# The activation tile in two column halves, one store on another queue, and eight small scalings in another place: an attention and gated feed-forward kernel

## The chip, the core and the metric

The kernel runs on one core of a Trainium2 chip. The metric is the device time of one execution in microseconds (us), the median of several runs. The core has a matrix engine (TensorE, PE in the profile, with its weight loads as PEld), VectorE (DVE), ScalarE (ACT), GpSimd (POOL) and SyncE (SP). SP, ACT and POOL can issue DMA transfers, each on a queue of its own; the profile calls these SPq, ACTq and POOLq.

## The reference, cut to what matters

Attention with a decay per head comes first, in blocks over the sequence; its output for all heads is then the input of a gated feed-forward layer.

```
B, H, S, D = 4, 8, 768, 64              # batches, heads, positions, width of a head
# attention, per block: qb, kb, vb; Dmask[i,j] = lam**(i-j) for i >= j, else 0
intra = ((qb @ kb.T) * Dmask) @ vb
inter = (qb * lam**(pos+1)) @ kv_state
out   = intra + inter
kv_state = lam**block * kv_state + (kb * lam**(block-1-pos)).T @ vb
# feed-forward, on x = out as [3072 tokens, 512]
gate = 1 / (1 + exp(-(x @ w_gate)))     # w_gate, w_val: [512, 1536]
val  = x @ w_val
y    = (gate * val) @ w_out             # w_out: [1536, 512], y in float32
```

The attention doesn't depend on the size of its blocks; the kernel takes blocks of 128 positions.

## The kernel before, in words

**Tiling.** The sequence is cut into six steps `n` of 128 positions, with all four batches side by side: 512 tokens in a step. For each step the attention leaves its result transposed in the tile `XT[n]`: 128 partitions (features of a head pair), four feature groups `m`, four batches `b`, 128 positions `c`. `XT` is bf16 and has two buffers.

**Attention of a step.** q and k are transposed (on PE with `t_`, copied out by `e_q` on DVE and `e_k` on ACT into `QS` and `KS`, L255; from step 2 on by DMA transposes, `xbar`, issued by SP). `piece_s` (L277) makes the scores `sp`, `piece_m` multiplies them by the decay mask on DVE, `piece_i` (L297) and `piece_a` (L308) make the output `op` from the state `Sb` and from v, `piece_x` (L318) copies `op` into `XT`, and `piece_c` (L326) makes the new state from v and the decayed keys `KD`. `piece_kd` (L125) makes these on ACT: one small scaling for each head and, in step 1, each half of the batches.

**Feed-forward of a step.** `piece_gv` (L343) makes one of twelve tiles of 128 hidden features: the gate product `gp` and the value product `vp`, each four matmuls over the feature groups (L353), a sigmoid on ACT (`sg`, L366), and the product `ht` on DVE (L371). `gp`, `vp` and the output product `po` rotate through three PSUM buffers. The first tile of steps 0 and 1 is made in halves of 256 columns, so that its first half needs batches 0 and 1 alone. `piece_po` (L386) then makes the output for one batch from the twelve `ht`, copies it to `ob` (L390) and, from step 1 on, issues its store at once (L376, on SP). Step 0's stores are issued later. The last output of all is made in two parts: columns 0 to 383 are copied by DVE, 384 to 511 by ACT, and each part has its store.

**Order.** The order of instructions on every engine is written out by hand: nothing is rescheduled. A list `plan` holds the feed-forward units, each with attention pieces that are recorded behind it; every engine works off its own instructions in the order of recording. Step 0's output products are split into the lower and upper six hidden tiles (`lo`, `hi`), with step 1's attention between them (L542 to L549). Weights arrive on POOL's queue, in groups of one or two tiles (`load_g`, `load_v`), and step 0's feed-forward begins while they still arrive.

**Around the change.** ACT's order from step 0's upper output products on is: output copy of batch 0, four decays, output copy of batch 1, four decays, output copy of batch 2, k copy `KS` of batches 2 and 3, four decays, output copy of batch 3, XT copies. PE's order there is: output products of batches 0, 1 and 2 (upper half), transposes of k and q, lower output products of batch 3, scores of batches 2 and 3, upper output products of batch 3, then the rest of step 1's attention.

Of the kernel before, what the change touches and what calls it, by code (L numbers as in the profile page):

```python
# [8 lines left out]
FP32 = mybir.dt.float32  # L9
BF16 = mybir.dt.bfloat16  # L10
AF = mybir.ActivationFunctionType
# [5 lines left out]
def kernel(  # L17
# [11 lines left out]
    nc = tc.nc  # L29

    B, H, S, D = q.shape
    C = 128
    NSTEP = S // C
    HP = H // 2
    DM = H * D
    DFF = moe_w_gate.shape[1]
    NFT = DFF // 128
    NMT = DM // 128
    TCH = B * C
# [9 lines left out]
    xtp = ctx.enter_context(tc.tile_pool(name="xtp", bufs=2))  # L49
    htp = ctx.enter_context(tc.tile_pool(name="htp", bufs=2))  # L50
# [4 lines left out]
    ps_ff = ctx.enter_context(tc.tile_pool(name="ps_ff", bufs=3, space=bass.MemoryType.PSUM))  # L55
# [4 lines left out]
    FIRST_XBAR = 2  # L60

    WG = const.tile([128, NMT, DFF], BF16, tag="WG")
    WV = const.tile([128, NMT, DFF], BF16, tag="WV")
# [56 lines left out]
    def piece_kd(n, hs, parts=(0, 1)):  # L120
        for h in hs:
            for bs in ((0, B),) if n == 0 else [((0, NB2), (NB2, B))[i] for i in parts]:
                at = slice(*bs)
                i = slot(n, bs[0], h)
                nc.scalar.mul(KD[n][:, at, i, :], T_["k", n][:, at, i, :], kds[:, h:h + 1])  # L125
# [100 lines left out]
    QS, KS, MT, XT, SP, OP = {}, {}, {}, {}, {}, {}  # L226
# [55 lines left out]
    def piece_m(n, b):  # L282
        MT[n, b] = mtp.tile([128, 2, HP, C], BF16, tag="MT", name="MT")
        for u in range(2):
            nc.vector.tensor_tensor(out=MT[n, b][:, u], in0=SP[n, b][u],  # L285
                                    in1=(mask if n else mask0)[:, 1 - u if swapped(n, b) else u],
                                    op=ALU.mult)
# [24 lines left out]

    def piece_x(n, bs, eng=None):
        if n not in XT:
            XT[n] = xtp.tile([128, NMT, B, C], BF16, tag="XT", name="XT")
        for b in bs:
            e = eng or (nc.vector if n < FIRST_XBAR and b >= NB2 else nc.scalar)
            (e.tensor_copy if e is nc.vector else e.copy)(XT[n][:, :, b, :], OP[n, b])  # L318

    def piece_c(n, hps):  # L320
        cp = ps_at.tile([128, len(hps), B, 64], FP32, name="cp", tag="ps")
# [19 lines left out]
    HT = {}  # L341

    def piece_gv(n, ft):  # L343
        fs = slice(ft * 128, (ft + 1) * 128)
        x = XT[n].rearrange("p m b c -> p m (b c)")
        gp = ps_ff.tile([128, TCH], FP32, name="gp", tag="ff")
        parts = [slice(0, TCH)]
        if n < FIRST_XBAR and ft == 0:
            parts = [slice(0, TCH // 2), slice(TCH // 2, TCH)]

        def product(ps, W, part):
            for mt in range(NMT):
                nc.tensor.matmul(ps[:, part], lhsT=W[:, mt, fs], rhs=x[:, mt, part],  # L353
                                 start=(part is parts[0] and mt == 0),
                                 stop=(part is parts[-1] and mt == NMT - 1), skip_group_check=True)

        product(gp, WG, parts[0])
        if n == 0 and ft == 0:
            product(gp, WG, parts[1])
            parts = [slice(0, TCH)]  # L360
        elif len(parts) == 2:
            vp = ps_ff.tile([128, TCH], FP32, name="vp", tag="ff")
            product(vp, WV, parts[0])
            product(gp, WG, parts[1])
        sg = htp.tile([128, TCH], BF16, tag="sg", name="sg", bufs=3)
        nc.scalar.activation(sg, gp, AF.Sigmoid)  # L366
        if len(parts) == 1:
            vp = ps_ff.tile([128, TCH], FP32, name="vp", tag="ff")
        product(vp, WV, parts[-1])
        HT[n, ft] = htp.tile([128, TCH], BF16, tag="ht", name="ht", bufs=2 * NFT)  # L370
        nc.vector.tensor_mul(HT[n, ft], sg, vp)  # L371

    OB, PO = {}, {}

    def store(n, tt, c0=0, c1=DM):
        nc.sync.dma_start(out=out[tt * S + n * C:tt * S + (n + 1) * C, c0:c1],  # L376
                          in_=OB[n, tt][:, c0:c1])

    def piece_po(n, tt, c0, c1, eng, fts):
        if (n, tt) not in OB:  # L380
            OB[n, tt] = osb.tile([128, DM], FP32, tag="ob", name="ob")
        if fts[0] == 0:
            PO[n, tt] = ps_ff.tile([128, DM], FP32, name="po", tag="ff")
        po = PO[n, tt]
        for ft in fts:
            nc.tensor.matmul(po[:, :c1 - c0], lhsT=HT[n, ft][:, tt * 128:(tt + 1) * 128],  # L386
                             rhs=WO[:, ft, c0:c1], start=(ft == 0), stop=(ft == NFT - 1))
        if fts[-1] == NFT - 1:
            o = OB[n, tt][:, c0:c1]
            (eng.copy if eng is nc.scalar else eng.tensor_copy)(o, po[:, :c1 - c0])  # L390
            if n:
                store(n, tt, c0, c1)
# [46 lines left out]
    for b in range(3):  # L439
        piece_a(0, [b])  # L440
        piece_x(0, [b], nc.vector if b == 2 else nc.scalar)
    swap_halves()
    ops = [ps_at.tile([128, HP // 2, C], FP32, name="op", tag="ps") for _ in range(2)]
    for g in range(2):
        for hp in range(2 * g, 2 * g + 2):
            for w in range(2):
                nc.tensor.matmul(ops[g][rows_of(w), hp % 2, :], lhsT=T_["v", 0][:, 3, 2 * hp + w, :],
                                 rhs=MT[0, 3][:, w, hp, :], start=(hp % 2 == 0), stop=(hp % 2 == 1),
                                 skip_group_check=True)
    nc.scalar.copy(XT[0][:, 0:2, 3, :], ops[0])  # L450
    nc.vector.tensor_copy(XT[0][:, 2:4, 3, :], ops[1])
    nc.vector.tensor_copy(lamqs, lqs[0])


# [35 lines left out]
    def unit(f, *more):  # L490
        plan.append((f, list(more)))

    def gv(n, ft, *more):
        unit(lambda: piece_gv(n, ft), *more)

    def po(n, tt, *more, c=(0, DM), eng=nc.scalar, fts=range(NFT)):
        unit(lambda: piece_po(n, tt, *c, eng, fts), *more)

    def pair(f, n, bp):
        return lambda: f(n, [2 * bp, 2 * bp + 1])  # L500

    def m_(n, b):
        return lambda: piece_m(n, b)

    def trans(n, bp):
        def go():
            bs = [2 * bp, 2 * bp + 1]
            t_("k", n, bs)
            e_k(n, bs)
            t_("q", n, bs)  # L510
            e_q(n, bs)
        return go
# [7 lines left out]
    def att(n):  # L520
        def go():
            piece_i(n)
            piece_a(n, range(B))
            piece_x(n, range(B))
            if n < NSTEP - 1:
                piece_c(n, [0, 1])
                piece_c(n, [2, 3])
        return go

    def kd(n, h0, h1=None, **kw):  # L530
        return lambda: piece_kd(n, range(h0, h1 or h0 + 2), **kw)
# [9 lines left out]
    lo, hi = range(NFT // 2), range(NFT // 2, NFT)  # L541
# [1 line left out]
    po(0, 1, trans(1, 0), fts=lo)  # L543
    po(0, 2, pair(piece_s, 1, 0), m_(1, 0), m_(1, 1), kd(1, 0, 4, parts=[0]), fts=lo)
    po(0, 0, kd(1, 4, 8, parts=[0]), fts=hi)
    po(0, 1, kd(1, 0, 4, parts=[1]), fts=hi)
    po(0, 2, trans(1, 1), fts=hi)
    po(0, 3, kd(1, 4, 8, parts=[1]), pair(piece_s, 1, 1), m_(1, 2), m_(1, 3), fts=lo)
    po(0, 3, att(1), fts=hi)  # L549

    for n in range(1, NSTEP):
# [13 lines left out]
        if n == 1:  # L565
            more[5:] = [more[3], more[4], more[5], [], more[7], more[8], []]
            more[3], more[4] = [], []
            for i in range(4):
                more[7 + i].append(kd(nx, 2 * i))
            more[11] = [att(nx)]  # L570
            more[2].append(lambda: next_loads(2))
            more[3].extend([lambda tt=tt, j=j: store(0, tt, 256 * j, 256 * j + 256)
                            for tt in range(B) for j in range(2)])
            more[8].append(lambda: next_loads(3))
# [44 lines left out]
```

## Time and profile before

| What | Value |
|---|---|
| Time, median of three runs | 227.84 us (227.43, 227.84, 227.85) |
| Time of the profiled execution | 227.5 us |
| Its span, first to last instruction | 225.5 us |
| Instructions | 4170 |
| PE busy | 219.0 us, 97% of the span |
| ACT busy | 101.7 us, 45% |
| DVE busy | 101.9 us, 45% |
| PE's granted clock | 1.000 |
| `gp` and `vp` products of 512 columns, each | 379 ns |
| Output copy on ACT, 128x512 | 586 ns |
| Last store: issue to landing | 1.9 us |

Busy time is the time in which an engine has an instruction at work. Matmuls follow each other before the one ahead has ended, so the 379 ns of a product is its length, not the distance to the next. "Idle before" in the profile is time in which an engine waited, with the instruction of another engine or the DMA that ended the wait. The chain of waits is followed back from the last instruction, at each step to what released it.

### The profile page before, as it was taken

The page shows a single profiled execution, that of the slowest core. Times are in us where ns is not written, and L with a number is a line of the kernel's source. Part 1 is how long each engine was busy: PE and PEld are TensorE (multiplying, and loading weights), DVE is VectorE, ACT ScalarE, POOL GpSimd, SP SyncE. Part 2 cuts the span into 40 slices and gives each one's busy share as a digit, 9 for nine tenths or more (in the row PEclk, how much of TensorE's full clock was granted, in tenths as well). Part 3 has the DMA queues.
Part 4 walks back from the last instruction along what each step waited for, and adds up shares of the span by engine and source line. Part 5 has one row for each costly group of instructions (what it writes and reads, how often), then busy time and mean ns, then how long its engine had stood idle before and what let it go on. Part 6 is the DMA issues. An engine that isn't in the chain of part 4 may idle for free.

```text
span 225.5 us, 4170 instructions
## 1 busy us (share of the span) xinstructions
PE 219.0 (97%) x1675; PEld 107.0 (47%) x1675; DVE 101.9 (45%) x187; ACT 101.7 (45%) x216; POOL 64.0 (28%) x83
## 2 busy tenths in 40 slices
PE   7899999999999999999999999999999999999993
PEld 2554444557444644444644444644444544444442
DVE  4774542548468801488410488420378400334200
ACT  5877433684348623348523348532332342333220
POOL 7999854740192049006600030000000000000000
PEclk9999999999999999999999999999999999999999
DMA  7999999999999959993993958012100012100022
GB/s 114 151 170 183 196 202 178 171 157 155 235 170 156 177 166 138 198 198 40 156 159 124 203 37 60 0 49 93 47 0 3 0 49 93 47 0 0 3 93 94
DMA packets 106003, 25.18 MB, mean 112 GB/s; under 512 B 97152, under 2 KB 103552, under 8 KB 105984
## 3 DMA queue, kind: packets, MB, share of 16 engines
q0 software_dynamic: 82944, 13.90, 80.1%
q1 hardware_dynamic: 22896, 11.01, 20.2%
q8 instruction: 13, 0.21, 0.4%
q14 instruction: 6, 0.05, 0.1%
q10 hardware_dynamic: 144, 0.00, 0.0%
HBM read 28.32 MB, written 6.29 MB: 153 GB/s over the span
## 4 chain that ended last, share of the span: by engine, by line
PE 88%; POOL 4%; DMA 3%; ACT 2%; issue 1%; POOLq 0%
PE vp L353 27%; PE gp L353 27%; PE po L386 26%; DMA WV<-in_moe_w_val_dram 3%; PE sp L277 2%; PE op L308 2%; POOL vb L92 1%; PE op L297 1%; PE cp L326 1%; ACT kd L125 1%; POOL qb L92 1%; ACT ob L390 1%; POOL WG L103 1%; POOL kb L92 1%; ACT KS L255 0%
## 5 line engine op out<-in xcount | busy, mean ns | idle before, releaser
L371 DVE TENSOR_TENSOR ht<-sg,vp 128x512 bf16<-128x512 bf16 x72 | 49.5, 687 | 94.5 <-PE vp L353 94.5
L353 PE MATMUL gp<-XT,WG 128*128 128x512 bf16 (+1 forms) x296 | 74.2, 374 | 0.3 <-ACT XT L450 0.3
L353 PE MATMUL vp<-XT,WV 128*128 128x512 bf16 (+1 forms) x292 | 74.1, 376 | 0.1
L366 ACT ACTIVATE sg<-gp 128x512 bf16<-128x512 f32 x72 | 43.0, 597 | 66.6 <-PE gp L353 65.5
L386 PE MATMUL po<-WO,ht 128*128 128x512 bf16 (+2 forms) x300 | 63.9, 371 | 0.0
L353 PEld LDWEIGHTS <-WV 128*128 128x128 bf16 x292 | 28.5, 98 | 33.7 <-DMA WV<-in_moe_w_val_dram 0.6
L353 PEld LDWEIGHTS <-WG 128*128 128x128 bf16 x296 | 28.2, 98 | 32.4 <-DMA WG<-in_moe_w_gate_dram 0.5
L386 PEld LDWEIGHTS <-ht 128*128 128x128 bf16 x300 | 28.3, 98 | 31.9
L390 ACT COPY ob<-po 128x512 f32<-128x512 f32 (+1 forms) x24 | 13.7, 571 | 42.1 <-PE po L386 40.1
L285 DVE TENSOR_TENSOR MT<-sp,mask 128x512 bf16<-128x512 f32 x48 | 30.4, 683 | 3.0 <-PE sp L277 3.0
L125 ACT ACTIVATE kd<-kb,kds 128x128 bf16<-128x128 bf16 (+1 forms) x72 | 23.9, 403 | 0.0
L477 POOL COPY gates<-kt 128x1 bf16<-128x1 bf16 x4 | 0.8, 188 | 50.5 <-DMA kt<-kb 50.5
L92 POOL DMA_DIRECT2D vb<-in_v_dram x9 | 11.9, 1334 | 3.0 <-issue 1.2
L318 ACT CAST XT<-op 128x512 bf16<-128x512 f32 x20 | 10.4, 597 | 5.1 <-PE op L308 5.1
L335 DVE SCALAR_TENSOR_TENSOR Sb<-Sb,dec,cp 128x128 bf16<-128x128 bf16 x32 | 8.6, 342 | 3.2 <-PE cp L326 3.2
L98 POOL DMA_DIRECT2D qb<-in_q_dram x10 | 8.9, 912 | 2.5 <-DMA WO<-in_moe_w_out_dram 2.5
L98 POOL DMA_DIRECT2D kb<-in_k_dram x10 | 8.9, 895 | 1.8 <-DMA WO<-in_moe_w_out_dram 0.6
L92 POOL DMA_DIRECT2D qb<-in_q_dram x8 | 9.0, 1128 | 1.0 <-POOLq L603 0.8
L400 PE MATMUL zps<-Sb 128*128 128x512 bf16 x18 | 7.1, 539 | 1.5 <-DVE Sb L152 1.5
L92 POOL DMA_DIRECT2D kb<-in_k_dram x6 | 7.0, 1160 | 1.1 <-DMA WO<-in_moe_w_out_dram 0.6
L106 POOL DMA_DIRECT2D WV<-in_moe_w_val_dram x9 | 7.2, 811 | 0.0
L103 POOL DMA_DIRECT2D WG<-in_moe_w_gate_dram x8 | 6.4, 799 | 0.5 <-issue 0.5
(59 smaller groups left out, 86.7 us busy)
## 6 DMA issues: line engine op xcount, KB each, us to landing
out_dram<-ob SPq DMA_DIRECT2D x19, 256.0 KB, 2.0
vb<-in_v_dram POOLq DMA_DIRECT2D x4, 512.0 KB, 7.6
qb<-in_q_dram POOLq DMA_DIRECT2D x6, 256.0 KB, 9.1
kb<-in_k_dram POOLq DMA_DIRECT2D x6, 256.0 KB, 8.2
qb<-in_q_dram POOLq DMA_DIRECT2D x12, 128.0 KB, 8.8
WO<-in_moe_w_out_dram POOLq DMA_DIRECT2D x4, 384.0 KB, 12.3
kb<-in_k_dram POOLq DMA_DIRECT2D x10, 128.0 KB, 8.8
WG<-in_moe_w_gate_dram POOLq DMA_DIRECT2D x4, 256.0 KB, 6.8
```

Source lines behind the costliest of these rows:

```text
L92: nc.gpsimd.dma_start(out=T_[c, n][:, b0:nat], in_=src[b0:nat, :, sl, :].rearrange("b h s d -> s (b h) d"))
L98: nc.gpsimd.dma_start(out=T_[c, n][:, m:b1, u::2, :], in_=src[m:b1, 1 - u::2, sl, :].rearrange("b h s d -> s (b h) d"))
L103: nc.gpsimd.dma_start(out=WG[:, :, f0 * 128:f1 * 128], in_=wg_r[:, :, f0 * 128:f1 * 128])
L125: nc.scalar.mul(KD[n][:, at, i, :], T_["k", n][:, at, i, :], kds[:, h:h + 1])
L285: nc.vector.tensor_tensor(out=MT[n, b][:, u], in0=SP[n, b][u], in1=(mask if n else mask0)[:, 1 - u if swapped(n, b) else u], op=ALU.mult)
L318: (e.tensor_copy if e is nc.vector else e.copy)(XT[n][:, :, b, :], OP[n, b])
L335: nc.vector.scalar_tensor_tensor(out=Sb[:, hp, at, :], in0=Sb[:, hp, at, :], scalar=d[:, hp:hp + 1], in1=cp[:, i, at, :], op0=ALU.mult, op ...
L353: nc.tensor.matmul(ps[:, part], lhsT=W[:, mt, fs], rhs=x[:, mt, part], start=(part is parts[0] and mt == 0), stop=(part is parts[-1] and m ...
L366: nc.scalar.activation(sg, gp, AF.Sigmoid)
L371: nc.vector.tensor_mul(HT[n, ft], sg, vp)
L386: nc.tensor.matmul(po[:, :c1 - c0], lhsT=HT[n, ft][:, tt * 128:(tt + 1) * 128], rhs=WO[:, ft, c0:c1], start=(ft == 0), stop=(ft == NFT - 1))
L390: (eng.copy if eng is nc.scalar else eng.tensor_copy)(o, po[:, :c1 - c0])
```

## The change

Three edits. `XT` becomes a tile of two column halves, each with its four feature groups: batches 0 and 1 lie in the first half, 2 and 3 in the second. A half product reads 256 columns that lie together, as before; a whole product reads two runs of 256 columns that are 1024 elements apart. `gp` and `vp` are declared in the same two halves, both ahead of the products, and `piece_gv` goes through a list of products; the order of matmuls stays. The store of the very last part (batch 3 of the last step, columns 384 to 511) is issued by ACT. The eight decays of batches 2 and 3 of step 1 are recorded together behind the lower output products of batch 3, and so behind the k copy of batches 2 and 3.

```
     def piece_x(n, bs, eng=None):
         if n not in XT:
-            XT[n] = xtp.tile([128, NMT, B, C], BF16, tag="XT", name="XT")
+            XT[n] = xtp.tile([128, 2, NMT, TCH // 2], BF16, tag="XT", name="XT")
         for b in bs:
             e = eng or (nc.vector if n < FIRST_XBAR and b >= NB2 else nc.scalar)
-            (e.tensor_copy if e is nc.vector else e.copy)(XT[n][:, :, b, :], OP[n, b])
+            (e.tensor_copy if e is nc.vector else e.copy)(
+                XT[n][:, b // 2, :, b % 2 * C:(b % 2 + 1) * C], OP[n, b])
...
     def piece_gv(n, ft):
         fs = slice(ft * 128, (ft + 1) * 128)
-        x = XT[n].rearrange("p m b c -> p m (b c)")
-        gp = ps_ff.tile([128, TCH], FP32, name="gp", tag="ff")
...
+        gp, vp = (ps_ff.tile([128, 2, TCH // 2], FP32, name=c, tag="ff") for c in ("gp", "vp"))
+        sg = htp.tile([128, TCH], BF16, tag="sg", name="sg", bufs=3)
+        whole, first, second = slice(0, 2), slice(0, 1), slice(1, 2)
 
         def product(ps, W, part):
             for mt in range(NMT):
...
+                nc.tensor.matmul(ps[:, part], lhsT=W[:, mt, fs], rhs=XT[n][:, part, mt],
+                                 start=(part is not second and mt == 0),
+                                 stop=(part is not first and mt == NMT - 1), skip_group_check=True)
+
+        order = [(gp, WG, whole), (vp, WV, whole)]
+        if ft == 0 and n == 0:
+            order = [(gp, WG, first), (gp, WG, second), (vp, WV, whole)]
+        elif ft == 0 and n == 1:
+            order = [(gp, WG, first), (vp, WV, first), (gp, WG, second), (vp, WV, second)]
+        for ps, W, part in order:
+            product(ps, W, part)
+            if ps is gp and part is not first:
+                nc.scalar.activation(sg, gp.rearrange("p a b -> p (a b)"), AF.Sigmoid)
...
     def store(n, tt, c0=0, c1=DM):
-        nc.sync.dma_start(out=out[tt * S + n * C:tt * S + (n + 1) * C, c0:c1],
+        (nc.scalar if (n, tt, c1) == (NSTEP - 1, B - 1, DM) else nc.sync).dma_start(out=out[tt * S + n * C:tt * S + (n + 1) * C, c0:c1],
                           in_=OB[n, tt][:, c0:c1])
...
-    nc.scalar.copy(XT[0][:, 0:2, 3, :], ops[0])
-    nc.vector.tensor_copy(XT[0][:, 2:4, 3, :], ops[1])
+    nc.scalar.copy(XT[0][:, 1, 0:2, C:], ops[0])
+    nc.vector.tensor_copy(XT[0][:, 1, 2:4, C:], ops[1])
...
-    po(0, 1, kd(1, 0, 4, parts=[1]), fts=hi)
+    po(0, 1, fts=hi)
     po(0, 2, trans(1, 1), fts=hi)
-    po(0, 3, kd(1, 4, 8, parts=[1]), pair(piece_s, 1, 1), m_(1, 2), m_(1, 3), fts=lo)
+    po(0, 3, kd(1, 0, 8, parts=[1]), pair(piece_s, 1, 1), m_(1, 2), m_(1, 3), fts=lo)
```

More of the change, by code (lines that the diff above doesn't have):

```diff
@@ L344, in piece_gv @@
         fs = slice(ft * 128, (ft + 1) * 128)
-        x = XT[n].rearrange("p m b c -> p m (b c)")
-        gp = ps_ff.tile([128, TCH], FP32, name="gp", tag="ff")
-        parts = [slice(0, TCH)]
-        if n < FIRST_XBAR and ft == 0:
-            parts = [slice(0, TCH // 2), slice(TCH // 2, TCH)]
+        gp, vp = (ps_ff.tile([128, 2, TCH // 2], FP32, name=c, tag="ff") for c in ("gp", "vp"))
+        sg = htp.tile([128, TCH], BF16, tag="sg", name="sg", bufs=3)
+        whole, first, second = slice(0, 2), slice(0, 1), slice(1, 2)
@@ L351, in product @@
         def product(ps, W, part):
             for mt in range(NMT):
[L353 to L369, printed above, removed]
+                nc.tensor.matmul(ps[:, part], lhsT=W[:, mt, fs], rhs=XT[n][:, part, mt],
+                                 start=(part is not second and mt == 0),
+                                 stop=(part is not first and mt == NMT - 1), skip_group_check=True)
@@ L370, in piece_gv @@
+        order = [(gp, WG, whole), (vp, WV, whole)]
[7 more added lines that the diff above has]
+                nc.scalar.activation(sg, gp.rearrange("p a b -> p (a b)"), AF.Sigmoid)
         HT[n, ft] = htp.tile([128, TCH], BF16, tag="ht", name="ht", bufs=2 * NFT)
-        nc.vector.tensor_mul(HT[n, ft], sg, vp)
+        nc.vector.tensor_mul(HT[n, ft], sg, vp.rearrange("p a b -> p (a b)"))
```

## The prediction

> **What bounds the kernel now.** I read the busy times first, then the list of PE's waits, then the chain of waits in order of time, and last the timeline of the two places that the chain points at.
>
> ```profile
> PE 219.0 (97%) x1675; PEld 107.0 (47%) x1675; DVE 101.9 (45%) x187; ACT 101.7 (45%) x216; POOL 64.0 (28%) x83
> PE zps L400 <- DVE Sb L152: 1.5, 1, 1.5
> PE sp L277 <- ACT KS L255: 0.5, 1, 0.5
> PE gp L353 <- ACT XT L450: 0.3, 1, 0.3
> PE tk L234 <- DVE kb L260: 0.2, 1, 0.2
> ```
>
> PE is busy for 219.0 of 225.5 us, and the other four lines are all the waits its matmuls have (us in total, times, longest). Three of them lie before 16 us. The table of stages says the same of the rest: between 48.6 and 221.9 us PE is busy for 173.26 of 173.30 us. So a gain can only come from ahead of 18 us, from the one wait near 48 us, from a matmul's own length, or from behind the last matmul.
>
> ```profile
> 12.11 5.84 DMA WV<-in_moe_w_val_dram
> 18.00 1.04 PE vp L353 x4
> ...
> 44.39 1.17 ACT kd L125 x4
> 45.56 0.47 ACT ob L390
> 46.03 1.18 ACT kd L125 x4
> 47.20 0.47 ACT ob L390
> 47.67 0.92 ACT KS L255
> 48.59 0.05 issue
> 48.64 0.62 PE sp L277 x16
> ```
>
> This is the chain of waits (start, length, what). The first two lines: the value product of the second feed-forward tile starts when its 128 columns of WV have landed, at 18.00, whatever PE did before. The last seven: at 44 to 48.6 the chain leaves PE and runs through ACT, because the k copy (KS) of batches 2 and 3 stands behind four key decays (kd) and two output copies.
>
> ```profile
> 47.29 0.69 DVE L244 TENSOR_TENSOR QS<-tq,lamq 128x1024 bf16<-128x1024 bf16 x1 [2.63 <-PE tq L234]
> ...
> 221.86 0.33 SPq L376 DMA_DIRECT2D out_dram<-ob  x1
> 221.94 0.27 ACT L390 COPY ob<-po 128x128 f32<-128x128 f32 x1 [2.03 <-PE po L386]
> ...
> 222.71 0.34 SPq L376 DMA_DIRECT2D out_dram<-ob  x1
> ```
>
> From the timeline. The q copy that the same scores need is ready at 47.98, ahead of KS (48.59). At the end the last output copy is done at 222.21, but its store leaves SP only at 222.71, since SP issued the store before it from 221.86 to 222.19.
>
> ```profile
> L353 PE MATMUL vp<-XT,WV 128*128 128x512 bf16 x284 | 72.9, 379 | 0.1
> L353 PE MATMUL gp<-XT,WG 128*128 128x512 bf16 x280 | 71.9, 379 | 0.0
> ```
>
> The groups kept apart by shape: 564 whole products are PE's largest work, and all read XT.
>
> [...]four products in 0.864 us, 216 ns each.[...] No operation of the kernel before moves data through PE in two runs[...].[...] SP's little semaphore instruction ends at 222.22, the copy it waits for at 222.21, and still 0.49 us pass before the store.[...]
>
> **The change, part by part.** Durations are of the profiled execution: span 225.5, time 227.5, so 2.0 us lie around the span. The median of the three runs shown is 227.84, 0.34 above it; I take the sum off the median.
>
> *Layout of XT.* It adds and removes no instruction. In the two built programs each half product waits for the same copies as before: the first four for ACT's second copy of XT, those of the second half for the copies of batches 2 and 3. Thus the layout takes no wait away. What it saves: nothing. Even if block 0's first tile began earlier, the cover is WV's landing at 18.00: PE starts the second gate product at 16.89, ends it 0.86 later at 17.75, and waits 0.25. If that cover were gone, the 0.30 us in front of the first product would be the most to gain. In block 1 the first half starts at 52.74 without a recorded wait. The XT copies write runs of 128 elements as before, with a smaller step between them; ACT's (597 ns, four runs) take what a sigmoid takes (597 ns, one run), so I cost those at nothing. What it may cost: 564 whole products now read two runs. Lower bound 0[...] . I take 0, as ACT's four-run writes pay nothing.
>
> *gp and vp as tiles of two halves, taken together.* The buffers rotate in the same order; the matmuls keep order and number. PE loses some waits on its own earlier matmuls and three small semaphore instructions, and gains a few such waits. All concern matmuls at least 28 PE instructions back, so done: 0 both ways.
>
> *k copies ahead of decays.* On ACT four kd (1.27 us) leave the place before the output copy of batch 2, and join the other four behind KS. New times: the 18 output products from 42.30 end as before; the last starts at 45.98 and ends 0.38 later at 46.36, so the output copy runs 46.40 to 46.99. The k transposes end at 46.80. KS, which overlaps the copy before it by 0.09, runs from 46.90 to 47.91, 0.68 earlier. PE needs it later than that: its last output product starts at 48.16, and elsewhere scores follow such a product by 0.305 (41.435 to 41.74). So scores start at 48.16 + 0.305 = 48.47 instead of 48.64, **0.17 us** earlier; the 0.5 in the list counts from another point. QS (47.98) and KS (47.91) both make it, with half a microsecond to spare. What is late next on ACT: eight kd of 0.29 to 0.32 from 47.8, done by 50.4. The next output copy, 50.70 before, is due at 50.53; the state products need the decays at 52.0. No DMA is moved past. Block 0's stores are issued from 59.24 on, behind SP's transposes, so earlier copies move none of them. Behind 48.6 PE has no other gap, so 0.17 reaches the end. Bounds: 0 to 0.17.
>
> *Last store on ACT's queue.* SP loses one issue and one semaphore instruction; ACT gains one issue behind its last copy, with nothing queued behind it but the end. On SP a store waiting for its copy left 0.03 after it (221.83 to 221.86). [...]the issue can start at 222.21 + 0.03 = 222.24: 0.47 earlier. Landing follows 1.9 after the start, and about 0.9 of closing follows that. Bytes follow an issue by 0.8 (the DMA rates show those of the 192 KB store from 222.7 to 223.4), so the small store's would start near 223.06 and share the last 0.3 us of those; I take 0.02 off: **0.45 us**. Floor: [...]222.21 + 0.49 = 222.70, gain 0. Below nothing: ACT's only earlier DMA took 0.43 to issue and 3.1 to land, against 0.34 and 1.9; 1.2 - 0.47 = 0.73 slower. I don't take it: that one was a broadcast load at the start beside two others, and SP's first issue took 0.46 as well. Ceiling: the 192 KB store lands at 221.86 + 1.9 = 223.76, 0.85 before the last one did.
>
> Sum: 0 + 0 - 0.17 - 0.45 = **-0.62 us**: 226.9 against the profiled 227.5, **227.2** against the median.
>
> **Rivals.**
> *The store gains nothing*[...]. For it: SP's 0.49 of silence. Against: SP had to issue another store right before. Then only 0.17 is left: 227.67. Chance 0.20.
> *The scores find another wait*, so that only the store counts: the output copy, now right behind its products, holds KS past 48.47. Against it speaks the half microsecond of room. 227.84 - 0.45 = 227.39, within the bound. Chance 0.10.
> *Two-run reads slow PE.* The place is each of the 564 whole products, with no cover as PE is full.[...] It cancels the gain at 0.62 / 564 = 1.1 ns and makes the kernel slower by 0.2% (0.46 us, about what a measurement can tell from no change) from 1.9 ns on. For it: XT's reads are the one thing changed in PE's bulk, and untried here. Against: ACT's strided writes are free. Chance 0.08.
> *The change does not do what it says*: the layout frees no wait, as shown; that is already in my forecast.
>
> **How the numbers follow.** My forecast has chance 0.62, at 227.2 with 227.0 to 227.4 of its own. Faster 0.62; the first two rivals make "within 0.2%", 0.30; the third slower, 0.08. The range 226.85 to 227.85 holds the forecast, both rivals inside 0.2%, and the 0.4 us by which the three runs shown differ; left out are the slow reads and part of the tails.
>
> **What would show it.** Right: whole gp and vp products still 216 ns apart; no wait of sp at L277 for KS, with kd x8 behind KS on ACT; the last store on ACT's queue at about the end of its copy, its landing near 224.2, a span near 224.9; 18.00 unchanged for the second value product. Wrong: a product spacing above 217 ns, an ACT store issued 0.4 us or more behind its copy, or landing later than 2.2 us, or a new PE wait behind 48 us.

## The result, and the profile after

The changed kernel takes 226.89 us, median of four runs (226.46 to 227.10), against 227.78 for the kernel before (four runs, 227.43 to 227.85). The ratio is 0.9962 with a 95% interval of 0.9944 to 0.9979: 0.89 us less by the medians, 0.5 to 1.3 by the interval. A second measurement gave 226.84 against 227.71, ratio 0.9956 (0.9943 to 0.9969). The profiled execution took 226.46 us with a span of 224.5, 1.0 us less than the span before. It was the fastest of its four runs, 0.43 under their median; the profiled execution before took 227.5, 0.28 under its own. So the two profiles overstate the gain by about 0.15 us. One execution of all those used below, one of the decays alone, took 582.44 us, and the figures of that kernel leave it out.

Lines of `piece_gv` and all behind it stand some lines further up in the changed file: L353 is L352 there, L386 is L381, L390 is L385, L376 is L371. First PE's busy time from the page, and the list of its matmuls' waits (us in total, times, longest), of the changed kernel.

```profile
PE 217.7 (97%) x1675; PEld 106.9 (48%) x1675; DVE 101.9 (45%) x187; ACT 101.7 (45%) x216; POOL 63.9 (28%) x83
PE zps L395 <- DVE Sb L152: 1.5, 1, 1.5
PE tq L234 <- DMA qb<-in_q_dram: 0.7, 1, 0.7
PE tk L234 <- DVE kb L260: 0.6, 1, 0.6
PE sp L277 <- ACT KS L255: 0.5, 1, 0.5
PE gp L352 <- ACT XT L445: 0.3, 1, 0.3
```

The line of `sp` and `KS` is still there. That is a correction to the prediction, which took it for the wait near 48 us. It is the wait of a much earlier `sp`, and was so before, so that all four waits listed in the prediction lie ahead of 16 us. This is the timeline of the kernel before at that place:

```profile
9.25 0.40 PE L277 MATMUL sp<-QS,KS 64*128 64x128 bf16 x8 [0.47 <-ACT KS L255]
```

The wait near 48 us stands with the weight loads, since the scores' weights are what comes from `KS`. The list of PEld's waits, first of the kernel before, then of the changed one:

```profile
PEld L277 <- ACT KS L255: 1.2, 2, 0.6
```

```profile
PEld L277 <- ACT KS L255: 0.6, 1, 0.6
PEld L277 <- ACT kd L125: 0.4, 1, 0.4
```

Of the two waits for `KS` one is left, and a line of 0.4 us with `kd` as its releaser has come in. The weight loads of the scores in question are these in the timeline, first before, then after:

```profile
48.63 0.45 PEld L277 LDWEIGHTS <-KS 64*128 64x128 bf16 x16 [0.58 <-ACT KS L255]
```

```profile
48.23 0.45 PEld L277 LDWEIGHTS <-KS 64*128 64x128 bf16 x16 [0.42 <-ACT kd L125]
```

The weight loads of the scores of batches 0 and 1, which in the kernel before wait for no other engine there, look like the second:

```profile
41.74 0.45 PEld L277 LDWEIGHTS <-KS 64*128 64x128 bf16 x16 [0.42 <-issue]
```

So 0.42 us passes there in any case. `kd` is named as the last thing on ACT by the profile, but these loads read `KS`, not `kd`, so I take it for no wait. What is gone is the rest, 0.58 - 0.42 = 0.16. The chain of waits of the changed kernel shows the place itself (start, length, what), and ACT's timeline beside it what ACT does there now.

```profile
46.12 0.45 PE tk L234 x8
46.56 0.45 PE tq L234 x8
47.01 1.29 PE po L381 x6
48.31 0.55 PE sp L277 x16
```

```profile
46.15 0.58 ACT L385 COPY ob<-po 128x512 f32<-128x512 f32 x1 [0.36 <-PE po L381]
46.64 1.02 ACT L255 COPY KS<-tk 128x1024 bf16<-128x1024 bf16 x1
47.54 2.44 ACT L125 ACTIVATE kd<-kb,kds 128x128 bf16<-128x128 bf16 x8
50.30 0.58 ACT L385 COPY ob<-po 128x512 f32<-128x512 f32 x1 [0.31 <-PE po L381]
```

The chain no longer leaves PE there: `KS` and the decays are gone from it. `KS` is done at 47.66, and the eight decays end at 49.98, before the next output copy is due. Whole products, which now read two runs, keep their distance, 0.86 us for four: first the chain before, then after.

```profile
23.35 0.86 PE vp L353 x4
24.21 0.86 PE gp L353 x4
```

```profile
55.11 0.86 PE vp L352 x4
55.97 0.86 PE gp L352 x4
```

At the end of the kernel, by the timeline:

```profile
221.46 0.33 SPq L371 DMA_DIRECT2D out_dram<-ob  x1
221.54 0.27 ACT L385 COPY ob<-po 128x128 f32<-128x128 f32 x1 [2.04 <-PE po L381]
221.84 0.35 ACTq L371 DMA_DIRECT2D out_dram<-ob  x1
```

The last store leaves 0.03 us behind its copy, where it left 0.50 behind it before.

**Where the 1.0 us of the two spans came from.** The last copy ends 0.40 earlier (221.81 for 222.21). Of this, 0.16 arose at the scores: from the first of the six lower output products to the scores it is 48.24 - 46.85 = 1.39, before 48.64 - 47.09 = 1.55. The other 0.24 was there ahead of them; the next section takes it for scatter of the first loads, not for a gain of the change. From the end of the last copy to the end of the span it is 2.72, before 3.29: 0.57. Together 0.40 + 0.57 = 0.97.

### The profile page after: what moved, and what is told of

The parts are those of the page before. It is cut to its first block, busy times and chain, and to the rows that moved or that the text cites. A ratio compares the mean times of both kernels' runs of the same rounds, so it can differ in the third digit from the quotient of the medians.

```text
span 224.5 us, 4166 instructions
## 1 busy us (share of the span) xinstructions
PE 217.7 (97%) x1675; PEld 106.9 (48%) x1675; DVE 101.9 (45%) x187; ACT 101.7 (45%) x216; POOL 63.9 (28%) x83
## 4 chain that ended last, share of the span: by engine, by line
PE 92%; POOL 3%; DMA 2%; issue 1%; ACT 0%; POOLq 0%
PE gp L352 28%; PE po L381 28%; PE vp L352 28%; PE sp L277 2%; DMA vb<-in_v_dram 2%; PE op L308 2%; PE op L297 1%; PE cp L327 1%; POOL qb L92 1%; POOL vb L92 1%; POOL kb L92 1%; PE tq L234 0%; PE tk L234 0%; ACT XT L445 0%; PE op L442 0%
## 5 line engine op out<-in xcount | busy, mean ns | idle before, releaser
L352 PE MATMUL gp<-XT,WG 128*128 128x512 bf16 (+1 forms) x296 | 74.2, 374 | 0.3 <-ACT XT L445 0.3
L352 PE MATMUL vp<-XT,WV 128*128 128x512 bf16 (+1 forms) x292 | 74.1, 376 | 0.0
L381 PE MATMUL po<-WO,ht 128*128 128x512 bf16 (+2 forms) x300 | 64.0, 371 | 0.0
L352 PEld LDWEIGHTS <-WV 128*128 128x128 bf16 x292 | 28.5, 98 | 33.6 <-DMA WV<-in_moe_w_val_dram 0.4
L352 PEld LDWEIGHTS <-WG 128*128 128x128 bf16 x296 | 28.2, 98 | 32.4 <-DMA WG<-in_moe_w_gate_dram 0.5
L381 PEld LDWEIGHTS <-ht 128*128 128x128 bf16 x300 | 28.3, 98 | 32.0 <-issue 0.2
L385 ACT COPY ob<-po 128x512 f32<-128x512 f32 (+1 forms) x24 | 13.7, 571 | 42.0 <-PE po L381 42.0
L395 PE MATMUL zps<-Sb 128*128 128x512 bf16 x18 | 6.3, 482 | 1.5 <-DVE Sb L152 1.5
```

The source lines that it names most:

```text
L352: nc.tensor.matmul(ps[:, part], lhsT=W[:, mt, fs], rhs=XT[n][:, part, mt], start=(part is not second and mt == 0), stop=(part is not first ...
```

## Experiments

Two questions were open: whether the layout has any part in the gain, and why the end of the kernel gave 0.57 where the earlier issue alone gives 0.47. Unless said otherwise each kernel is compared with the kernel before on the same chip in five rounds.

### The layout alone

The kernel before with the first edit only (XT, gp and vp in two halves; store on SP, decays as before).

> The kernel before with the column halves of XT, gp and vp alone; store on SP and decays as before. My theory (the layout takes no wait away and two-run reads are free): 0 us, within 0.15 of the kernel before; whole products still 216 ns apart (four in 0.86 us); the last store on SP still about 0.5 us behind its copy; scores at L277 still held by KS. Rival A (the layout is what brought the 0.3 us that the sum did not hold): 0.25 to 0.3 us faster. Rival B (two-run reads cost): slower, 0.56 us for each ns a product.

Measured: 227.68 against 227.71 us, ratio 0.9995 (0.9985 to 1.0004). It is worth nothing that can be told: the interval goes from 0.34 us faster to 0.09 slower. Whole products keep their 0.86 us for four. Its second value product started at 18.34, *later* than the kernel before's 18.00, and in the changed kernel it started at 17.69. Over the profiles with the new layout the start is 18.34, 17.69, 17.81 and 17.97 (the last with XT in four runs, a kernel further down); over those without it, 18.00, 18.11, 17.97, 17.99, 17.97 and 18.09. In eight of these ten profiles the start waits for the landing of WV, which is at 17.64 in the changed kernel's and at 17.77 to 18.06 in the others; in two (the layout alone, 18.34, and all but the layout, 18.09) WV landed earlier, at 17.90 and 17.66, and the start waits for the products ahead of it, which were late behind the landing of a block of v. So the start follows when the first loads land, and it scatters by some 0.6 us; WV landed at 17.66 without the layout too. I take the 0.24 in front of the scores for this scatter. Rival B is out. Rival A's 0.25 to 0.3 us lies just inside the interval; its start should have been earlier, and this profile shows it later.

### The store alone

```
     def store(n, tt, c0=0, c1=DM):
-        nc.sync.dma_start(
+        (nc.scalar if (n, tt, c1) == (NSTEP - 1, B - 1, DM) else nc.sync).dma_start(
...
```

> The kernel before with the last store alone on ACT's queue. My theory: the store starts 0.03 us behind its copy instead of 0.50, so 0.45 to 0.5 us faster. Rival A: the closing behind the store also gets shorter (0.13 us in the profile of the changed kernel), so 0.6 us faster. Rival B: part of the gain is lost to the transfer that it now overlaps: 0.3 us or less.

Measured: 227.06 against 227.71 us, ratio 0.9969 (0.9957 to 0.9981), so 0.65 us less (0.43 to 0.98 by the interval, whose lower end is about the predicted 0.45). The store starts at 222.35, 0.03 behind its copy, and from the end of the copy to the end of the span it is 2.74 us, before 3.29: 0.55, so that more than the start shortened, as rival A had it. The store starts where the prediction had it; the size of the gain was put too small.

### The decays alone

```
-    po(0, 1, kd(1, 0, 4, parts=[1]), fts=hi)
+    po(0, 1, fts=hi)
     po(0, 2, trans(1, 1), fts=hi)
-    po(0, 3, kd(1, 4, 8, parts=[1]), pair(piece_s, 1, 1), m_(1, 2), m_(1, 3), fts=lo)
+    po(0, 3, kd(1, 0, 8, parts=[1]), pair(piece_s, 1, 1), m_(1, 2), m_(1, 3), fts=lo)
```

> The kernel before with the eight decays behind the k copy alone. My theory: scores start 0.30 to 0.31 us behind the last output product instead of 0.48, so 0.16 to 0.17 us faster, and no more. Rival: by being earlier the rest of step 1 on ACT frees something else, 0.3 us or more; then PE would show another gap closed behind 48 us.

Measured: 227.59 (thirteen runs) against 227.71 us, ratio 0.9993 (0.9984 to 1.0001). By the ratio 0.16 us, by the medians 0.12: the time agrees with the theory, and with nothing as well. The trace is clearer: from the first lower output product to the scores it is 1.40 us (47.05 to 48.45), as in the changed kernel, where the two kernels above without this edit have 1.55 and 1.54. No other gap behind 48 us closes.

### The changed kernel again

> The changed kernel once more, unchanged. My theory: the parts add to 0.62 to 0.65 us, and the 0.89 of the first measurement held some 0.25 of scatter of the landing of the first loads: 0.55 to 0.75 us faster here. Rival: the extra is real, 0.85 us or more.

Measured: 226.84 against 227.71 us, ratio 0.9956 (0.9943 to 0.9969): 0.87 us. This expectation failed, and its rival held: the interval, 0.71 to 1.30 us, leaves out 0.62. The three parts measured alone add to 0.03 + 0.65 + 0.12 = 0.80 by medians, and most of what the prediction lacked is in the store.

### All but the layout

The kernel before with both the store and the decays.

> The kernel before with the store on ACT's queue and the decays behind the k copy, and XT, gp and vp as before: all of the change but the layout. The changed kernel was 0.87 us faster than the kernel before in its second measurement (interval 0.71 to 1.3). Theory (the layout is worth nothing, also beside the others): 0.75 to 0.9 us faster, ratio 0.996 to 0.9967. Rival (the layout helps only once the rest is in place): 0.6 us faster or less.

Measured: 227.00 against 227.79 us, ratio 0.9964 (0.9950 to 0.9977): 0.79 us, within what the theory gave. Its interval, 0.52 to 1.14, holds the rival's 0.6 as well. The layout adds nothing that these intervals can tell beside the other two edits either.

### The two last stores with queues exchanged

Is SP itself slow, or is it SP with another issue just behind it? SP here issues the small store alone; ACT issues the large one.

```
-            if n:
+            if n and (n, tt, c1) != (NSTEP - 1, B - 1, 384):
                 store(n, tt, c0, c1)
+            if (n, tt, c1) == (NSTEP - 1, B - 1, DM):
+                store(n, tt, 0, 384)
...
-        nc.sync.dma_start(
+        (nc.scalar if c1 == 384 else nc.sync).dma_start(
...
```

> The kernel before with the queues of the two last stores exchanged: SP issues the small one (64 KB) and, with no other issue ahead of it in the last microsecond, ACT issues the larger one (192 KB) behind its own last copy. Theory[...]: SP's small store starts 0.02 to 0.05 us behind its copy. Rival: SP is slow by itself, 0.4 us or more. As to the time: the 192 KB now start about 0.4 us later than before, beside the 64 KB; [...]the gain is below that of the store alone: 0 to 0.4 us faster.

Measured: 227.08 against 227.87 us, ratio 0.9970 (0.9959 to 0.9981): as good as the store on ACT. The timeline of the end:

```profile
221.94 0.27 ACT L390 COPY ob<-po 128x128 f32<-128x128 f32 x1 [2.03 <-PE po L386]
221.94 0.35 ACTq L376 DMA_DIRECT2D out_dram<-ob  x1
222.23 0.33 SPq L376 DMA_DIRECT2D out_dram<-ob  x1
```

SP's store starts at 222.23, 0.02 behind its copy (222.21). So SP is not slow by itself: this store has no other issue of SP just ahead of it, where in the kernel before 0.52 us passed behind the large store's (222.19 to 222.71). One issue behind another does not take that long everywhere: among the eight stores of step 0, from 59.24 us on in the kernel before, 0.04 to 0.10 us lies between the end of one issue and the start of the next. What sets the 0.52 was not shown. My guess on the large store was wrong: ACT does not hold it until its own copy is done. It starts together with that copy at 221.94, 0.08 later than SP issued it before and not 0.4, so this run could not show whether a late large store lands late as well.

### The store late on ACT's queue

The store alone, but ACT makes its last copy three times, so that the store leaves as late as SP's did.

```
-            (eng.copy if eng is nc.scalar else eng.tensor_copy)(o, po[:, :c1 - c0])
+            for _ in range(3 if (n, tt, c1) == (NSTEP - 1, B - 1, DM) and c0 else 1):
+                (eng.copy if eng is nc.scalar else eng.tensor_copy)(o, po[:, :c1 - c0])
```

> The kernel before with the last store on ACT's queue, and ACT's last output copy made three times over, so that the store is issued 0.5 to 0.65 us behind the end of the first of them: no earlier than SP issued it (0.50), but on ACT's queue. The store alone was 0.65 us faster than the kernel before; its earlier start explains 0.47 of it. Theory A (the rest is time[...]): landing is 1.9 to 2.2 us again, and the time 0.05 to 0.2 us slower than the kernel before. Theory B (the rest is the queue: ACT's lands faster): landing 1.8, and the time within 0.05 us of the kernel before, or faster.

Measured: 227.57 against 227.83 us, ratio 0.9991 (0.9985 to 0.9998). The profile sides with theory A: the store starts at 222.81, 0.62 behind the end of the first copy (222.18), and lands after 1.9 us again; from the end of the first copy to the end of the span it is 3.46 us, and the kernel before and the two kernels with a late SP store (layout alone, decays alone) have 3.29, 3.44 and 3.58. The time does not quite: 0.2 us less than the kernel before by the ratio (0.05 to 0.34), where theory A had it slower. So ACT's queue may still be worth 0.1 or 0.2 us by itself; this is open. Against it speaks the run before this one, which gained as much with the small store on SP.

The DMA view gives the time from issue to landing (median; each line is one store). The decays alone, the late store on ACT, the exchanged queues and the changed kernel, in this order:

```profile
out_dram<-ob SPq DMA_DIRECT2D x1, 64.0 KB, 2.2
```

```profile
out_dram<-ob ACTq DMA_DIRECT2D x1, 64.0 KB, 1.9
```

```profile
out_dram<-ob SPq DMA_DIRECT2D x1, 64.0 KB, 1.8
```

```profile
out_dram<-ob ACTq DMA_DIRECT2D x1, 64.0 KB, 1.8
```

Landing was 1.8 when the store left early, on either queue, and 1.9 to 2.2 when it left late, on either queue. The trace has 16 completions of each of these stores, and the landing is the last of them (in the kernel before at 224.60, 1.89 behind the issue at 222.71). Their times show what lands late:

| Kernel | Queue | Issue behind the (first) copy | Landing | Last completion behind the 15th |
|---|---|---|---|---|
| before | SP | 0.50 | 1.9 | 0.28 |
| layout alone | SP | 0.50 | 2.0 | 0.45 |
| decays alone | SP | 0.49 | 2.2 | 0.53 |
| late on ACT | ACT | 0.62 | 1.9 | 0.26 |
| exchanged | SP | 0.02 | 1.8 | 0.01 |
| store alone | ACT | 0.03 | 1.8 | 0.01 |
| changed | ACT | 0.03 | 1.8 | 0.02 |
| changed, again | ACT | 0.03 | 1.8 | 0.00 |
| all but layout | ACT | 0.03 | 1.8 | 0.08 |

In the four kernels whose store left late, the last completion of sixteen came 0.26 to 0.53 us behind the 15th; in the five others 0.00 to 0.08. What is beside it then? The DMA view of the kernel before, in the stretch from 223.3 to 224.1 us in which the small store's packets run (queue, kind: packets, MB, share of 16 engines):

```profile
q1 hardware_dynamic: 148, 0.07, 28.5%
q14 instruction: 1, 0.01, 4.1%
```

And of the changed kernel, from 223.1 to 223.7, with ACT's queue as q10:

```profile
q14 instruction: 1, 0.01, 5.4%
q10 hardware_dynamic: 16, 0.00, 2.8%
```

Every profile of the table has this one instruction packet of 8 KB there. In the kernel before it runs from 223.33 for 0.52 us, and the store's packets from 223.55 to 224.04; in the changed kernel it runs from 223.13, when the store's (222.82 to 223.18) are all but through. It starts 1.1 to 1.5 us behind the end of the copy in the three kernels whose store leaves late on SP's queue. So a late store's packets ran beside it, and an early one's for 0.08 us at most. Whether this packet has a part in the late completion was not shown: the records used here don't name each packet's engine.

### XT in four runs, and at steps of seven and four elements

These ask where the rival of slow reads would have begun. All three start from the changed kernel and had one run each. First, one run for each batch: `xtp.tile([128, B, NMT, C])`, read as `XT[n][:, b0:b1, mt]`.

> The changed kernel with XT laid out by batch, so that a whole product reads four runs of 128 columns instead of two of 256, and a half product two. My theory (runs are free): four whole products still in 0.86 us, time as the changed kernel (226.5 to 227.1). Rival (each break costs): 0.5 us or more slower.

Measured: 226.72 us, as the changed kernel. The groups by shape:

```profile
L352 PE MATMUL vp<-XT,WV 128*128 128x512 bf16 x284 | 72.9, 379 | 0.0
L352 PE MATMUL gp<-XT,WG 128*128 128x512 bf16 x280 | 71.9, 379 | 0.0
```

The same lengths as in the kernel before. Runs of 128 columns cost PE nothing here that can be told. Then steps: `xtp.tile([128, TCH, 7])`, with column c of group m at element 7 c + m, and the same with 4.

> The changed kernel with XT laid out so that the columns of a product lie seven elements (14 bytes) apart[...], and the XT copies write at that step. It bounds when the way PE reads XT does matter. [...]whole products more than 216 ns apart[...]. Rival (PE reads any step at full rate): 216 ns, time within 1 us of the changed kernel; the XT copies may take longer[...].

> The changed kernel with XT laid out so that the columns of a product lie four elements (8 bytes) apart[...]; a step of seven took 0.785 us a product instead of 0.216. Theory[...]: whole products 216 ns apart, time within 1 us of the changed kernel but for longer XT copies. Rival (any step costs): products between 0.25 and 0.8 us apart, 20 us or more slower.

Measured: 575.34 us at a step of seven, 366.93 at four. From the timeline of the step of seven, at two places:

```profile
302.44 3.33 PE L352 MATMUL vp<-XT,WV 128*128 128x512 bf16 x4
305.58 3.33 PE L352 MATMUL gp<-XT,WG 128*128 128x512 bf16 x4
...
308.73 3.33 PE L352 MATMUL vp<-XT,WV 128*128 128x512 bf16 x4
311.88 3.33 PE L352 MATMUL gp<-XT,WG 128*128 128x512 bf16 x4
```

Four products take 305.58 - 302.44 = 3.14 us, 0.785 each, 3.6 times the 0.216 of columns that lie together. At a step of four:

```profile
230.81 1.99 PE L352 MATMUL gp<-XT,WG 128*128 128x512 bf16 x4
232.62 1.99 PE L352 MATMUL vp<-XT,WV 128*128 128x512 bf16 x4
```

That is 1.81 / 4 = 0.45 each, 2.1 times. PE's granted clock fell to 0.598 on average in the first of the two, but was 0.991 in the second. The clock is not the cause of the longer products: from 300 to 304 us it was 1.00, from 308 to 312 it was 0.50, and in these stretches four products took 3.14 and 3.15 us. The copies that write XT slowed as well (medians, from no step to four and seven): on ACT from 0.59 to 1.40 and 2.44 us, on DVE from 0.68 to 1.30 and 2.14. So the theory for the step of four, products 216 ns apart, failed, and its rival, 0.25 to 0.8 us, held.

No version in these runs beats the changed kernel beyond its interval.

## Why the prediction was right, point by point

The prediction was 227.2 us, 0.62 less than before, within 226.85 to 227.85; the time was 226.89, near the lower end. Faster was given 0.62. That it fell inside the range owes something to luck: the second measurement, 226.84, lies just outside, and both lie below the 227.0 to 227.4 that the prediction gave to its own forecast. The places and their causes were right, one size was not.

- **PE without gaps, so only the ends and one place count.** Right: 97% before and after, and no other wait moved behind 48 us.
- **Layout: 0.** Right for the reason given, as far as the intervals tell. It frees no wait, and reads in two runs keep PE's pace, 0.86 us for four products; in four runs a product has the same 379 ns. Slow reads do exist, 0.45 us a product at a step of four elements and 0.785 at seven, but this layout has no such step.
- **18.00 unchanged.** Wrong as a mark to look for: this start scatters from 17.69 to 18.34 between profiles with the landing of the first loads. In the changed kernel's profile it added 0.31 at that place, 0.24 of it left at 46 us, to a difference of two single executions.
- **Decays: 0.17.** Right: 0.16 by the trace, and the time alone couldn't show it. `KS` was reckoned done at 47.91 with PE as before, and came at 47.66 with PE 0.24 ahead, which is the same. The wait list was misread on the way: its 0.5 us are those of 9.25. The sum didn't use them, as it went by the distance of the starts.
- **Store: 0.45.** The start was right to the hundredth, 0.03 behind the copy. (SP's semaphore instruction ended at 222.25, not 222.22, so 0.46 us of silence followed it, not 0.49; nothing hangs on it.) The term mis-sized is the landing, taken as 1.9 both before and after: it measured 1.8 against 1.9 to 2.2, and the store alone was worth 0.65. From the end of the copy to the end of the span it is 3.29, 3.44 and 3.58 us in the three profiles with a late store on SP, and 2.72 to 2.81 in five with an early one on ACT (the store alone, the changed kernel twice, all but the layout, XT in four runs): 3.44 against 2.75 on average. That is 0.69, and with the 0.16 of the decays 0.85, where 0.89 and 0.87 were measured. What the landing loses is the one late completion of sixteen, 0.26 to 0.53 us behind the others when the store left late and 0.00 to 0.08 when it left early; what makes it late was not shown. The small store's first packet came 0.98 behind its issue in the changed kernel, where the large store's packets still ran, and 0.83 before. If that 0.15 is the overlap, taken as 0.02, the shorter landing outweighs it.
- **The span near 224.9.** 224.5 in the profile, 224.9 in the middle of the runs.
- **Rivals.** "The store gains nothing" is refuted by the store alone. "The scores find another wait" did not come about either: the 0.42 us ahead of their weight loads is what loads without a wait show too.

## What to carry to other kernels

Look at the last issue of a kernel against the end of what it stores: if its queue has just issued something else, as SP had here until 222.19 for a copy that ended at 222.21, a queue that has nothing to do may save that time; here it didn't matter which of the two stores was moved to it (ratios 0.9969 and 0.9970). With PE busy for 97% of the span, the wait showed itself as a longer distance between two starts, 1.55 us for 1.39, and stood with the weight loads, 0.58 us for 0.42; so compare such a distance with the same pair elsewhere, and look at the weight loads' waits, not at the matmuls' alone. The operand that a matmul streams cost nothing more here in two runs of 256 or four of 128 columns (379 ns a product in both); at a step of four or seven elements the products that read it stood 0.45 and 0.785 us apart instead of 0.216.

## What the runs showed of the hardware that I had not expected

One of a store's 16 completions came 0.26 to 0.53 us behind the others in all four kernels whose last store left about half a microsecond late, beside an instruction packet of 8 KB that took 0.3 to 0.5 us; that the packet is the cause was not shown. In the five other profiles of the table, whose store left at once, it was 0.00 to 0.08.

PE's granted clock of 0.50 did not lengthen products that read at a step of seven elements: 0.79 us each at 0.50 (308 to 312 us) and at 1.00 (300 to 304 us).

The two steps fit one simple price, an estimate from these two points: 0.4525 / 4 = 0.113 and 0.785 / 7 = 0.112 us a product for each element of the step. At a step of one that would be 0.11 us, where columns that lie together took 0.216, so the price does not reach down to them. Two points can't tell what it is a price of.
